# Second-half queries by seven block products (Strassen's scheme), with weight sums and split K and V kept in DRAM

## The chip, the core and the metric

The kernel runs on one core of one Trainium2 chip. The metric is the device time of one execution in microseconds (us), taken as the median of several executions. Below, PE is TensorE (the matrix engine; PEld is its loading of weights), DVE is VectorE, ACT is ScalarE, POOL is GpSimd, and SP is SyncE, which in this kernel does nothing but issue DMAs.

## What is computed

```python
def _A_ref(x, k_cache, v_cache, wq, wo):          # x: 2048 x 640; 32 heads of 128
    q = (x @ wq).reshape(B, Sq, 32, 128)...
    k = k_cache[:, :, Sk - W:, :]                 # the last W = 512 positions
    v = v_cache[:, :, Sk - W:, :]
    p = softmax(einsum("bhqd,bhkd->bhqk", q, k) * 128 ** -0.5)
    o = einsum("bhqk,bhkd->bhqd", p, v)
    return o.transpose(...).reshape(B, Sq, 4096) @ wo
def _B_ref(x, w1, b1, w2, b2):                    # 640 -> 1728 -> 640
    r = maximum(x @ w1 + b1, 0)
    return (r * r) @ w2 + b2
xn = layernorm(x)
return x + _A_ref(xn, ...) * silu(_B_ref(xn, ...))
```

All arrays are float32. Every matrix product is made from three products of a high and a low part: a = ah + al, b = bh + bl, and a·b is taken as ah·bh + ah·bl + al·bh. The high part is a copy rounded to the matrix engine's float32r (an ACT copy), the low part is the difference (a subtraction on DVE or POOL). So each 128x128 block of weights against 512 tokens costs three matmul instructions.

## The kernel before

**Stages.** The 2048 tokens are four tiles of 512. The first three go through the layer norm and the MLP (`mlp_step`, one step for each of 14 chunks of the hidden layer in each tile); the split, normalised x of all tiles is put in DRAM (`xT_d`). The MLP of the fourth tile (LATE) is done at the very end, under and behind the last attention units. Between them stands attention: 128 units, in two halves of 64. A half holds two token tiles; in it the 16 groups of two heads are gone through, and for each group the four units (token tile 0, heads 0 and 1; token tile 1, heads 0 and 1). Below, u0 to u3 are these four places, so that unit number modulo 4 is the place.

**One unit** is, on PE, 12 matmuls of scores (`s_mm`, tile s), 15 of the query of two units later (`q_mm`, tile pq; 5 chunks of the 640 inputs, three matmuls each), 12 of the weighted sum of V of the unit before (`v_mm`, tile o), and, on average, 15 of the output projection of earlier units (`r_mm`, tile r): 54.

**The loop through one unit.** The scores of a unit lie in four PSUM banks. DVE takes the maximum over the keys for each query (three folds, tile rdm); ACT gathers four strips (`gather`); DVE finishes the maximum (sqm) and turns it (rowm); SP writes the 2 KB row to DRAM (m_d) and, when that has landed, loads it back, spread over 128 partitions (bm, `row`). DVE then subtracts bm from the scores into SBUF (`shift`, tile e), which frees the banks for the scores of the next unit. ACT takes the exponential and its high part (`expo`, `p_hi`), POOL makes the low part (`p_lo`) and the sum of the two halves (`s_add`, tile su). DVE folds the sums (rds, sqs, rows), which go by DRAM as well (s_d, bs), and in the unit after next the sum of V is scaled by them (`o_norm`), split (`o_hi` on ACT, `o_lo` on DVE: tile ot) and used by `r_mm`. The o bank is single: the next `v_mm` waits for `o_lo`. A DVE instruction `r_acc` adds each projected piece to acc.

**What sets the order.** The attention's instructions are recorded in a plan: `at(when, f, ...)`, sorted by `when`, with a nominal unit (`PERIOD`) of 12.4. It sets only the order in which each engine's instructions stand; every engine then goes through its own in order. All loads and stores of the attention, m_d, bm, s_d and bs among them, are issued by SP in that one order. In a unit SP issues, in this order: m_d, bm, s_d (the sums), bs, and then loads for later units: before, two of raw weights, of 256 or 320 KB (vr, kr, qr, or for V, K and the two weights), which ACT and POOL split into high and low parts when they have landed (`load_raw`, `prep`). Each head's K, V, query weights and output weights are loaded and split in both halves, so twice in all. In units 73 to 112 `load_finish` adds one transfer of 256 KB in each unit (fs, fx, fg, then a store) for the final combination of the first half's tokens.

At the change of halves, units 60 to 64, the x of the second half's two tiles is loaded chunk by chunk (`load_xT`, tile ax).

## Time and profile before

| what | value |
| --- | --- |
| time, median of 3 runs | 1992.19 us (1991.41 to 1992.53) |
| the profiled execution | 1990.35 us, of which the span from first to last instruction is 1988.6 us |
| PE busy | 1958.7 us, 98% of the span, 8576 matmuls recorded |
| DVE, POOL, ACT busy | 1515.5 (76%), 1375.3 (69%), 1186.3 us (60%) |
| granted TensorE clock, mean | 0.999 |
| DMA | 220.39 MB, mean 111 GB/s |
| attention | first scores at 307.1 us, last unit's scores at 1879 us |

Busy time is an average over stages; in the middle of attention PE is busy without a gap. A view of the trace by stretches of time gives busy times and counts of instructions of each engine in each stretch, with the share of the 16 DMA engines' time that was busy and what they moved. The timeline lists instructions by start, each with its duration, merged where equal ones follow each other (x3), and in brackets the idle time of the engine just before and what ended it. "SPq" is SP's queue: a row there is the issue of a DMA, not its transfer.

### The profile page before, as it was taken

The numbers are of one execution on the slowest core, as the hardware profiler recorded it, in microseconds if no ns is written. First come the engines' busy times: TensorE is split into PE (matmuls) and PEld (weight loads), VectorE is DVE, ScalarE is ACT, GpSimd is POOL, SyncE is SP. The second block draws the span as 40 slices with busy tenths as digits, with TensorE's granted clock in tenths as the row PEclk, the third lists the DMA queues.
The fourth block names the chain that finished last, engine by engine and source line by source line (L and its number), as shares of the span: only waits on it lengthen the run. The fifth ranks groups of instructions, "written<-read, shape, count | busy, mean of one in ns | idle before, by whom it ended". The sixth has DMA issues, their size and how long they took to land.

```text
span 1988.6 us, 25917 instructions
## 1 busy us (share of the span) xinstructions
PE 1958.7 (98%) x8576; PEld 1603.1 (81%) x8576; DVE 1515.5 (76%) x2511; ACT 1186.3 (60%) x2034; POOL 1375.3 (69%) x755
## 2 busy tenths in 40 slices
PE   7999999999999999999999999999999999999998
PEld 6788887788888888888887788888888888888877
DVE  5523236788888888888888878888888888888864
ACT  4432326766666666666666676666666666666643
POOL 1121225888888888888887788888888888888841
PEclk9999999999999999999999999999999999999999
DMA  4421444322323233222335433333333333333354
GB/s 137 136 106 38 180 171 144 105 91 94 95 93 91 91 91 91 91 90 92 94 93 170 157 98 107 112 112 113 112 112 115 113 112 113 96 91 91 110 147 141
DMA packets 126871, 220.39 MB, mean 111 GB/s; under 512 B 21542, under 2 KB 36304, under 8 KB 125456
## 3 DMA queue, kind: packets, MB, share of 16 engines
q1 hardware_dynamic: 123744, 204.28, 32.9%
q0 software_dynamic: 2992, 14.43, 1.8%
q8 instruction: 69, 1.13, 0.2%
q14 instruction: 66, 0.54, 0.1%
HBM read 194.26 MB, written 24.39 MB: 110 GB/s over the span
## 4 chain that ended last, share of the span: by engine, by line
PE 88%; DMA 4%; DVE 4%; ACT 2%; issue 1%; POOL 1%; SPq 0%; POOLq 0%; DVEq 0%; ACTq 0%
PE pq L72 20%; PE r L72 20%; PE o L72 17%; PE s L72 17%; PE py L96 2%; PE py L97 2%; PE py L95 2%; PE ph L97 2%; PE ph L96 2%; PE ph L95 2%; PE ly L72 2%; PE lu L72 1%; DMA w1r<-in_w_dram 1%; DMA bm<-m_d 1%; DVE rdm L72 1%
## 5 line engine op out<-in xcount | busy, mean ns | idle before, releaser
L72 POOL TENSOR_TENSOR pt<-e,pt 128x1024 fp32r<-128x1024 f32 x256 | 616.2, 2407 | 120.4 <-ACT pt L72 120.4
L72 PE MATMUL r<-ot,wo 128*128 128x512 f32 x1920 | 496.9, 389 | 0.2 <-DVE acc L72 0.2
L72 PE MATMUL pq<-ax,wq 128*128 128x512 f32 x1920 | 456.6, 389 | 0.8 <-DMA ax<-xT_d 0.7
L72 PEld LDWEIGHTS pq<-ax,wq 128*128 128x128 f32 x1920 | 360.6, 188 | 76.3 <-DMA ax<-xT_d 1.5
L72 PEld LDWEIGHTS r<-ot,wo 128*128 128x128 f32 x1920 | 360.3, 188 | 75.6 <-DVE acc L72 0.6
L72 PE MATMUL s<-q,wk 128*128 128x512 f32 x1536 | 372.1, 391 | 5.9 <-DVE e L72 5.9
L72 PE MATMUL o<-pt,wv 128*128 128x512 f32 x1536 | 374.6, 392 | 1.4 <-DVE ot L72 1.2
L72 ACT ACTIVATE e<-e 128x1024 f32<-128x1024 f32 x256 | 269.9, 1054 | 126.0 <-DVE e L72 122.1
L72 PEld LDWEIGHTS s<-q,wk 128*128 128x128 f32 x1536 | 287.9, 188 | 70.7 <-issue 7.2
L72 PEld LDWEIGHTS o<-pt,wv 128*128 128x128 f32 x1536 | 283.5, 188 | 72.9 <-DVE ot L72 14.9
L72 DVE TRANSPOSE_TENSOR_REDUCE rdm<-s 128x16 f32<-128x512 f32 (+1 forms) x384 | 313.4, 868 | 36.9 <-PE s L72 36.2
L72 DVE TENSOR_TENSOR e<-s,bm 128x512 f32<-128x512 f32 (+1 forms) x384 | 304.3, 842 | 17.0 <-DMA bm<-m_d 16.8
L72 POOL TENSOR_TENSOR su<-e,e 128x1024 f32<-128x1024 f32 x128 | 307.6, 2403 | 0.0
L72 ACT ACTIVATE pt<-e 128x1024 fp32r<-128x1024 f32 x256 | 272.0, 1062 | 7.9
L237 POOL TENSOR_TENSOR r<-r 128x512 f32<-128x512 f32 (+1 forms) x42 | 44.1, 1051 | 227.9 <-ACT r L278 208.8
L72 DVE TENSOR_TENSOR acc<-r,acc 128x512 f32<-128x512 f32 x300 | 198.6, 662 | 2.7 <-PE r L72 2.7
L72 ACT ACTIVATE ot<-o 128x512 fp32r<-128x512 f32 x128 | 76.8, 600 | 197.1 <-DVE o L72 197.1
L72 ACT ACTIVATE rds<-rds 32x32 f32<-32x32 f32 x384 | 87.7, 228 | 128.5 <-DVE rds L72 125.5
L72 DVE TRANSPOSE_TENSOR_REDUCE rds<-su 128x32 f32<-128x1024 f32 x128 | 158.1, 1235 | 0.1
L72 DVE TENSOR_TENSOR ot<-o,ot 128x512 fp32r<-128x512 f32 x128 | 88.6, 692 | 85.2 <-ACT ot L72 85.2
L72 POOL TENSOR_TENSOR wv<-vr,wv 128x512 fp32r<-128x512 f32 x64 | 83.2, 1300 | 81.5 <-ACT wv L72 74.4
L72 POOL TENSOR_TENSOR wq<-qr,wq 128x640 fp32r<-128x640 f32 x62 | 97.7, 1576 | 60.2 <-ACT wq L72 60.2
(123 smaller groups left out, 2168.6 us busy)
## 6 DMA issues: line engine op xcount, KB each, us to landing
bm<-m_d SPq DMA_DIRECT2D x128, 256.0 KB, 3.2
bs<-s_d SPq DMA_DIRECT2D x128, 256.0 KB, 3.8
qr<-in_wq_dram SPq DMA_DIRECT2D x64, 320.0 KB, 4.1
or<-in_wo_dram SPq DMA_DIRECT2D x64, 320.0 KB, 4.1
kr<-in_kT_dram SPq DMA_DIRECT2D x64, 256.0 KB, 3.4
vr<-in_v_dram SPq DMA_DIRECT2D x64, 256.0 KB, 4.3
xT_d<-xT POOLq DMA_DIRECT2D x6, 1280.0 KB, 7.5
xb<-in_x_dram SPq DMA_DIRECT2D x16, 320.0 KB, 3.4
```

The lines of the kernel that those rows point to most:

```text
L72: ins = method(*args, **kwargs)
L95: nc.tensor.matmul(ps, ah, bh, start=first and i == 0, stop=False)
L96: nc.tensor.matmul(ps, ah, bl, start=False, stop=False)
L97: nc.tensor.matmul(ps, al, bh, start=False, stop=last and i == n - 1)
L237: nc.gpsimd.tensor_tensor(r, r, r, op=ALU.mult)
```

## The change

**In the second half** the 15-matmul query products are replaced. For a group, the four wanted blocks (two heads by two token tiles) over the first four chunks of the 640 inputs form a 2x2 by 2x2 block product; it is made with seven block products in place of eight (`PRODUCTS`, `part`), each of 2 chunks x 3 matmuls. The fifth chunk is added straight (four times 3 matmuls). So a group takes 54 matmuls for its queries where it took 60; over 16 groups that is 96 fewer, and 8482 in place of 8578 in the program. The factors are sums and differences of weight blocks (segments A to D, tiles ws) and of x blocks (four tiles t). The products are joined by three copies on ACT (`snap`), four additions of PSUM to SBUF on DVE (`joined`) and three on POOL (`mixed`); the split of the joined query is an ACT copy and a POOL subtraction (`joined_hi`, `joined_lo`), where before the latter was on DVE (`q_lo`, 64 of them are gone).

**In the first half** each group's weight sums are made, by five subtractions or additions of two SBUF operands on DVE (`combos`, written to cs), a copy on ACT and a subtraction on POOL (`combos_hi`, `combos_lo`), and they, the split query weights, and the split K and V of each head are stored to DRAM (`store_q`, `store_s`, `store_kv`: w_d and kv_d). The second half loads them split (`load_seg`, `load_kv`, 512 or 640 KB each) instead of loading raw and splitting anew. At the end of the first MLP the sums and differences of the x of the last two tiles are made and stored (`t_prep`: 16 POOL, 8 DVE and 8 ACT instructions on 128x512, 16 stores of 256 KB); the layer norm of the last tile is put one step earlier (`LN_AT`).

**Elsewhere**: the output weights are loaded as five pieces of 128 KB a group (`load_o`, `prep_o`); `s_add` becomes two additions within the halves, and the second `p_lo` is cut in two; e, pt, bm and bs have one buffer less; the r pieces of the second half stand at other places (`r_plan`), since its units have 51, 51, 54 and 54 matmuls; at the change of halves nine blocks of x and of its sums are loaded, in transfers of 256 or 512 KB.

SP's order, first half, from the bs of unit 32 (a u0) to the m_d and bm of unit 33 (a u1), and on to that unit's bs. Names: m_d the row of maxima and bm its copy over all partitions, s_d and bs the same of the sums; vr, qr, or raw loads of V, query and output weights; sizes in elements. Before:

```order
L72 DMA bs_6500<-s_d_6498 128x512
L72 DMA vr_17_6514<-in_v_dram 128x512
L72 DMA qr_18_6516<-in_wq_dram 128x640
L72 DMA m_d_6576<-rowm_6574 16x32
L72 DMA bm_6578<-m_d_6576 128x512
L72 DMA s_d_6626<-rows_6624 16x32
L72 DMA bs_6628<-s_d_6626 128x512
```

Now, from the bs to the m_d of unit 33 (kv_d and w_d are the new stores):

```order
L72 DMA bs_6985<-s_d_6983 128x512
L72 DMA kv_d_164<-wk_17_6846 128x1024
L72 DMA vr_17_7005<-in_v_dram 128x512
L72 DMA qr_7007<-in_wq_dram 128x640
L72 DMA w_d8A<-co_6950 256x1x256
L72 DMA w_d8B<-co_6950 256x1x256 x2
L72 DMA w_d8C<-co_6950 256x1x256
L72 DMA w_d8C<-cs_6651 256x1x128
L72 DMA m_d_7073<-rowm_7071 16x32
```

Two transfers stood between a bs and the next m_d, eight stand there now (512, 256, 320, four of 256 and one of 128 KB).

SP's order, second half, late, from the bs of unit 119 (a u3) to the m_d of unit 120 (a u0), and on. Names: as above, and wk, wv the split K and V, ws31A a segment of the weight sums. Before:

```order
L72 DMA bs_17762<-s_d_17760 128x512
L72 DMA vr_28_17776<-in_v_dram 128x512
L72 DMA or_28_17778<-in_wo_dram 128x640
L72 DMA m_d_17837<-rowm_17835 16x32
L72 DMA bm_17839<-m_d_17837 128x512
L72 DMA s_d_17888<-rows_17886 16x32
L72 DMA bs_17890<-s_d_17888 128x512
```

and now:

```order
L72 DMA bs_18725<-s_d_18723 128x512
L72 DMA or_3_18744<-in_wo_dram 128x2x128
L72 DMA wk_29_18746<-kv_d_176 128x1024
L72 DMA or_4_18753<-in_wo_dram 128x2x128
L72 DMA ws31A<-w_d15A 128x2x512
L72 DMA wv_28_18788<-kv_d_175 128x1024
L72 DMA m_d_18818<-rowm_18816 16x32
```

Two raw loads became five, 1792 KB in all.

DVE's order, second half, in unit 120 (a u0), from its folds to the split of o. Names: rdm the folded maxima of the scores s, sqm and rowm the row, acc the projected output, o and ot the sum of V and its low part. Before:

```order
L72 TENSOR_REDUCE rdm_17810<-s_0_17794 128x2x16
L72 TENSOR_REDUCE rdm_17810<-s_2_17805 128x16
L72 TENSOR_REDUCE rdm_17810<-s_3_17813 128x16
L72 TENSOR_REDUCE sqm_2330<-rdm_17810 32x16
L72 STREAM_TRANSPOSE rowm_17835<-sqm_2330 32x32
L72 TENSOR_TENSOR acc_0_11050<-r_1_17821,acc_0_11050 128x512
L72 TENSOR_TENSOR o_17764<-o_17764,bs_17762 128x512
L72 TENSOR_TENSOR ot_17847<-o_17764,ot_17847 128x512
```

Now, in the same unit (sn is a partial query in SBUF, ps the bank of the block products):

```order
L72 TENSOR_REDUCE rdm_18785<-s_0_18766 128x2x16
L72 TENSOR_REDUCE rdm_18785<-s_2_18780 128x16
L72 TENSOR_REDUCE rdm_18785<-s_3_18790 128x16
L72 TENSOR_TENSOR acc_0_11910<-r_0_18757,acc_0_11910 128x512
L72 TENSOR_TENSOR sn_7_18553<-ps_4_18708,sn_7_18553 128x512
L72 TENSOR_REDUCE sqm_2504<-rdm_18785 32x16
L72 STREAM_TRANSPOSE rowm_18816<-sqm_2504 32x32
L72 TENSOR_TENSOR o_18727<-o_18727,bs_18725 128x512
L72 TENSOR_TENSOR acc_0_11910<-r_1_18805,acc_0_11910 128x512
L72 TENSOR_TENSOR ot_18827<-o_18727,ot_18827 128x512
```

Before, the row (sqm, rowm) followed the folds at once, with one `acc` behind it; now an `acc` and a joining addition stand between the folds and the row, and the other `acc` stands between o and ot.

The core of the diff:

```diff
-                if n or kind in "vo":
-                    at(base + when - 10.5, load_raw, kind, hf, h)
-                    at(base + when, prep, kind, hf, h)
+                if hf == 0:
+                    if n or kind == "v":
+                        at(base + when - 10.5, load_raw, kind, hf, h)
+                        at(base + when, prep, kind, hf, h)
+                    if kind != "q":
+                        at(base + when + (13.6 if n or kind == "v" else 27.0 + j), store_kv, kind, h)
+                elif kind == "k":
+                    at(base + (j - 2) * PERIOD + 9.9, load_kv, kind, h)
+                elif kind == "v":
+                    at(base + j * PERIOD + 2.0, load_kv, kind, h)
...
+        if hf == 0:
+            at(base + c0, combos, g, (0,))
+            at(base + c1, combos, g, (1, 2))
+            at(base + c2, combos, g, (3, 4))
+            at(base + 6.0, combos_hi, g)
+            at(base + 9.8, combos_lo, g)
+            for j in range(G):
+                at(base + (0.0 if n == 0 else (j - 2) * PERIOD) + 2.0, store_q, g, j)
+            at(base + PERIOD + 2.0, store_s, g)
+        else:
+            for k, s in enumerate("ABCD"):
+                at(base + (k - 4) * PERIOD + 0.3, load_seg, n, s)
...
+    PRODUCTS = {
+        1: (("A", 0, ("x", 1, 0)),),
+        6: (("A", 2, ("t", 1)),),
+        7: (("B", 0, ("t", 2)),),
+        5: (("B", 2, ("t", 0)), ("B", 4, ("x", 0, 2))),
+        3: (("C", 0, ("x", 0, 1)), ("C", 2, ("x", 0, 2))),
+        4: (("C", 3, ("t", 3)),),
+        40: (("D", 0, ("x", 1, 2)),),
+        2: (("D", 1, ("x", 1, 1)), ("D", 3, ("x", 1, 2))),
+    }
...
+    def store_kv(kind, h):
+        sp.dma_start(kv_d[h][:, int(kind == "v")], raw({"k": KT, "v": VV}[kind][0, h]))
+    def load_kv(kind, h):
+        sp.dma_start(raw(open_kv(kind, 1, h)), kv_d[h][:, int(kind == "v")])
...
+            dve.tensor_tensor(out, a, b, op=ALU.subtract if k else ALU.add)
```

More of the change, by code (lines that the diff above doesn't have):

```diff
@@ L45 @@
     LATE = NTILE - 1
-    LN_AT = {t: (3, 7) if t == LATE else (5, 9) for t in range(1, NTILE)}
+    LN_AT = {t: (2, 6) if t == LATE else (5, 9) for t in range(1, NTILE)}
     SCALE = DH**-0.5
@@ L846 @@
+    at(10.0, pad, pools["ep"], 480)
+    for m, k, when in (
+        (("x", 1, 0), -4, 0.6),
+        (("t", 2), -4, 4.6),
+        (("t", 1), -4, 9.9),
+        (("x", 0, 2), -3, 0.6),
+        (("t", 0), -3, 9.9),
+        (("t", 3), -2, 0.6),
+        (("x", 1, 2), -2, 4.6),
+        (("x", 0, 1), -2, 9.9),
+        (("x", 1, 1), -1, 0.6),
+    ):
+        for i in range(2):
+            at((DU + k) * PERIOD + when + 0.1 * i, load_x, 1, m, i)
     R_AT = (
@@ L857, with r_plan @@
     R_BANK, R_BANK_END = (1, 0, 0, 1, 0), (1, 1, 1, 0, 0)
+    R_BANK_ST = (1, 0, 1, 0, 0)
+    def r_plan(i, d):
+        if i == NU - G - 1:
+            (when, js) = R_AT_END[d][0]
+            return ((when, js),), R_BANK_END[d], when + 0.68 * len(js)
+        if i + 2 < DU - 3 or i + 4 > NU - 3:
+            pieces = R_AT[d]
+            when, js = pieces[-1]
+            return pieces, R_BANK[d], when + 0.68 * len(js)
+        x = (i + 3) % UPG == 2
+        two, three, four = (k * PERIOD for k in (2, 3, 4))
+        return (
+            (((two + 11.3, range(G)),), 1, three + 3.9),
+            (((three + (4.1 if x else 3.5), range(G)),), 0, three + (5.7 if x else 5.1)),
+            (
+                ((three + (5.5 if x else 4.8), range(1)), (four + (4.8 if x else 4.1), range(1, G))),
+                1,
+                four + (5.8 if x else 5.1),
+            ),
+            (((three + 11.3, range(G)),), 0, four + 0.3),
+            (((four + (5.5 if x else 4.8), range(G)),), 0, four + (7.0 if x else 6.3)),
+        )[d]
     for i in range(NU):
@@ L889 @@
         on(PERIOD + 8.5, row, i, "s")
-        on(18.6, p_lo, i, 1)
         for c in range(KC):
```

431 lines of the change are left out of this document (321 added, 110 removed).

## The prediction

> **What bounds the kernel now.** First the page's busy times, queues and costliest groups, then the view by stretches of time, one long stretch late in the second half and one about the change of halves.
>
> ```profile
> PE 1958.7 (98%) x8576; PEld 1603.1 (81%) x8576; DVE 1515.5 (76%) x2511; ACT 1186.3 (60%) x2034; POOL 1375.3 (69%) x755
> q1 hardware_dynamic: 123744, 204.28, 32.9%
> ...
> 1046.80:1162.10 115.30, 112.16 (x488) 90.62 (x487) 94.10 (x156) 73.42 (x129) 89.37 (x46) 1.00 0.48 154
> 1608.00:1803.00 195.00, 195.00 (x858) 160.13 (x857) 167.84 (x280) 127.13 (x224) 160.47 (x82) 1.00 0.33 103
> ```
>
> PE is busy all of 195 us with 858 matmuls: 0.2273 us each, at a granted clock of 1.00. A unit of 54 takes 12.27 us. So matmuls bound the middle of attention, and fewer of them is worth time only as long as nothing else takes a unit's length. What stands next is the loop through DRAM. The timeline of a usual unit, SP and PE rows, then some of DVE's:
>
> ```profile
> 1507.79 0.32 SPq L72 DMA_DIRECT2D bs<-s_d  x1
> 1507.99 2.88 PE L72 MATMUL s<-q,wk 128*128 128x512 f32 x12
> 1508.23 0.35 SPq L72 DMA_DIRECT2D vr<-in_v_dram  x1
> 1508.63 0.43 SPq L72 DMA_DIRECT2D qr<-in_wq_dram  x1
> 1509.47 0.33 SPq L72 DMA_DIRECT2D fs<-s_d  x1
> 1513.52 0.33 SPq L72 DMA_DIRECT2D m_d<-rowm  x1
> 1514.84 0.33 SPq L72 DMA_DIRECT2D bm<-m_d  x1
> 1516.15 2.88 PE L72 MATMUL o<-pt,wv 128*128 128x512 f32 x12
> 1520.23 1.07 PE L72 MATMUL s<-q,wk 128*128 128x512 f32 x4
> ...
> 1513.29 0.20 DVE L72 STREAM_TRANSPOSE rowm<-sqm 32x32 f32<-32x32 f32 x1
> 1513.43 0.66 DVE L72 TENSOR_TENSOR o<-o,bs 128x512 f32<-128x512 f32 x1
> 1514.75 0.69 DVE L72 TENSOR_TENSOR ot<-o,ot 128x512 fp32r<-128x512 f32 x1 [0.67 <-ACT ot L72]
> 1518.38 1.77 DVE L72 TENSOR_TENSOR e<-s,bm 128x1024 f32<-128x1024 f32 x2
> ```
>
> From scores to scores 12.24 us. bm can be issued only when m_d has landed, here 1.32 us after its issue and 6.85 us after the scores began. The subtraction starts at 10.39, gives up the first two banks (1024 of the 1536 columns that the row's 1.77 us cover, 1.18) at 11.57, and PE wants them at 12.24: 0.67 us of slack. The transfers ahead of m_d here are bs and three loads, 832 KB. The DMA view gives the sizes; kr, fs and bs are of 256 KB like vr, or of 320 like qr:
>
> ```profile
> qr<-in_wq_dram SPq DMA_DIRECT2D x64, 320.0 KB, 4.1
> vr<-in_v_dram SPq DMA_DIRECT2D x64, 256.0 KB, 4.3
> ax<-xT_d SPq DMA_DIRECT2D x20, 256.0 KB, 5.0
> ```
>
> Where more stood ahead, the kernel already pays. Two units near the change of halves, one with five loads ahead (by the same view three ax, vr and or, 1344 KB), one with six (1600 KB):
>
> ```profile
> 1046.81 2.88 PE L72 MATMUL s<-q,wk 128*128 128x512 f32 x12
> 1054.72 0.32 SPq L72 DMA_DIRECT2D bm<-m_d  x1
> 1059.48 0.70 PE L72 MATMUL s<-q,wk 128*128 128x512 f32 x2 [0.20 <-DVE e L72]
> ...
> 1085.01 2.88 PE L72 MATMUL s<-q,wk 128*128 128x512 f32 x12
> 1085.20 0.86 SPq L72 DMA_DIRECT2D ax<-xT_d  x2
> 1086.34 0.33 SPq L72 DMA_DIRECT2D kr<-in_kT_dram  x1
> 1086.72 0.42 SPq L72 DMA_DIRECT2D or<-in_wo_dram  x1
> 1087.19 1.17 SPq L72 DMA_DIRECT2D ax<-xT_d  x2
> 1090.54 0.32 SPq L72 DMA_DIRECT2D m_d<-rowm  x1
> 1093.72 0.32 SPq L72 DMA_DIRECT2D bm<-m_d  x1
> 1097.16 2.42 DVE L72 TENSOR_TENSOR e<-s,bm 128x1024 f32<-128x1024 f32 x3 [1.70 <-DMA bm<-m_d]
> 1098.53 0.70 PE L72 MATMUL s<-q,wk 128*128 128x512 f32 x2 [1.12 <-DVE e L72]
> ```
>
> m_d is issued in time (in the second 5.53 us after the scores, as above) but lands behind the loads: bm goes out at 7.91 and 8.71, and the units take 12.67 and 13.52 us, bm's time plus 4.8 in both. 256 KB more cost 0.80 us, 3.1 us per 1000 KB. The queue's own row agrees: 204.28 MB in 32.9% of 1988.6 us is 312 GB/s, 3.2 us per 1000 KB. So m_d has a price list: by a usual unit's slack 832 KB are as good as free, 1344 KB cost 0.4 us and 1600 KB cost 1.25, with 3.1 us for each further 1000 KB. The Trainium skill (DMA: Bandwidth & Descriptors, Queues, rings and completion order) says that each DMA engine takes descriptors in the order of its ring; by that rule a 2 KB row waits for all that is ahead, and the trace agrees.
>
> **The change part by part.** *Matmuls.* 96 x 0.2273 = 21.8 us less on PE, all in the second half, in the places u0 and u1 (51 matmuls, 11.59 us). But there the o product stands after 33 matmuls, 7.50 us, where it stood after 36 (8.16 in the row). It needs the o bank: ot ends 7.45 us after the scores in the rows above (1515.44), with only one `acc` between the folds and the row. In u0 two additions stand there, and in u1 two come ahead of the folds; of 0.6 us each, the gather's gap takes most, some 0.25 stays. So the product starts about 7.94 (ot's end at 7.7, and the load of weights behind it), 0.44 late, in 31 units: +13.6. Left of the saving: 8 us.
>
> *SP's queue, first half.* By the order, the transfers between a bs and the next m_d are 1024 KB in u0, 2240 in u1, 1728 in u2 and 1664 in u3; before, 576. From the 1600 KB unit: u1 has 640 KB more, 2.0 us, so bm at 10.7 and a unit of 15.5 (+3.2). u2 would be 13.9, but a long u1 lets bs and the loads start some 1.5 us earlier against u2's scores: +0.1. u3: 13.7 (+1.4). u0: nothing. Sum 4.7 for four units. One unit is little ground, and the stores of K and V move 4 KB a row, which may drain faster than 2; with 1 us less in u1 and u3 the sum is 2.5 or so. Nearest is the 1600 KB row, for u3 nearly the same load, so I keep between the ends: 3.6. Units 5 to 59 are 13.75 such fours: 49 us (34 to 65). No cover is left, since the slack is used before.
>
> *DVE against POOL, first half.* The five `combos` read two SBUF operands each and stand between the folds and the row. Such an operation is seen beside POOL here:
>
> ```profile
> 326.89 2.41 POOL L72 TENSOR_TENSOR pt<-e,pt 128x1024 fp32r<-128x1024 f32 x1
> ...
> 328.14 1.71 DVE L72 TENSOR_TENSOR eh_g<-lr,eh_x 128x512 fp32r<-128x512 f32 x1
> ```
>
> It takes 1.71 us and ends 0.55 after POOL's (329.30), where DVE's o and ot above, of the same 128x512, take 0.66 and 0.69. So it waits for the running POOL operation, up to 2.4 us. The Trainium skill (SBUF — State Buffer, SBUF: two separate sides) calls this an exclusive lock between GpSimd and a VectorE operation with two SBUF inputs; the row agrees. In u3 the wait lies under the queue's, in u2 under slack; in u0 it shows. I take 0.5 us for four units, 7 us (0 to 27: 2 us). POOL itself gets 45.4 us of work in four units of 49.1, against 40.4. With 2.41 for 1024 columns from the row above, this one gives the scale, 2.16 us per 1000 columns and 0.2:
>
> ```profile
> L72 POOL TENSOR_TENSOR wv<-vr,wv 128x512 fp32r<-128x512 f32 x64 | 83.2, 1300 | 81.5 <-ACT wv L72 74.4
> ```
>
> (Four `p_lo` of 2.41 and eight halves of 1.30, eight sums of 1.30, raw weights 8.4, five pieces of 256 columns at 0.75, and 2.9 for the low part of the weight sums.) It fits, a u0 that runs 1 us over being made good in u1; cost nothing, and up to 1 us a four if that cover is gone.
>
> *SP's queue, second half.* Ahead of m_d stand 1792 KB in u0, 1152 in u1, 768 in u2, 1280 in u3. u0: bm at 8.71 + 0.6 = 9.3, unit 14.1, 2.1 over the 12.0 that the o bank gives. u3: +0.25. With the finish transfers of 256 KB (10 of 15 fours) u0 gets 2.5 (0.8 more, less 0.4 since u3 is longer) and u3 1.05; I take off 0.25 for what 832 KB cost before. That is 2.35 or 3.3; with 0.7 to 1 us less, 1.4 or 1.9. Middle: 1.9 x 5 + 2.6 x 10 = +35 (26 to 45).
>
> *The rest.* Change of halves, units 60 to 64: 18.7 MB are queued in place of 9.5, 9.2 x 3.1 = 28 us of transfer, of which about half falls into time in which the queue stood idle (0.48 busy there before): +12 (3 to 25). First units, where 2176 to 2752 KB stand ahead of m_d three times: +5 (0 to 10). `t_prep`: POOL gets 5.2 us (four of 1.30) a step of 30 matmuls, 6.8 us, beside its square: +2 (0 to 8). ACT has a third of its time free, and the single buffers of bm and bs are free in time by the rows above: nothing.
>
> Sum: -21.8 + 13.6 + 49 + 7 + 35 + 12 + 5 + 2 = +102. The profiled execution took 1990.35 us, which gives 2092; the median of the runs stands 1.84 above it: **2094 us**. The ends, added up (with half of the o wait at the low one): 2040 and 2164.
>
> By the skill's ceiling of 435 GB/s for the 16 engines (same page, Specifications), 2.3 us per 1000 KB, u1 of the first half would be 0.5 shorter and the estimate some 10 us lower; no stretch of this trace shows that rate.
>
> **The rivals.** *The queue hides it* (faster): if the larger rows drain so fast that up to 2.2 MB pass ahead of m_d in the slack, only PE and the o bank count: 1992 - 8 = 1984. It decides at m_d's landing by 7 us. For it: even about the change of halves the engines are idle for half the time (0.48 busy for 154 GB/s). Against: in that very stretch 1600 KB put bm at 8.71. 10%.
> *Half-way* (slower): only u1 in the first half and u0 in the second pay, 1 us each: 1992 - 8 + 14 + 15 + 8 = 2021. For it: the price list rests on two units. Against: the queue's own rate gives the same price. 15%.
> *POOL becomes the bound*: if the lock stalls POOL as well, its 45.4 us grow past the longer fours (52.7) and e and pt, with two buffers, hold back the subtraction: each `combos` then costs its full 2.4, 12 us a four, 165 us more than I count, about 2250. Only one row shows the lock in attention. 6%.
>
> **How the numbers follow.** The forecast, 2040 to 2164, has 69%. The range takes in most of the half-way case and cuts the top: 2010 to 2150. Runs here differ by 1 us, so 0.2% (4 us) is about what can be told from no change. Faster 0.10, the first rival; the same 0.02, the border of the two; slower 0.88.
>
> **What would show it.** Right: bm issued 9 us or more after the scores in u1 (first half) and u0 (second half), waits of DVE's e for bm as in the row of 1097.16 (1.70 us) in two of four units, PE's s waiting for e, and 3 to 5 us per four in the first half, where no matmul changed. Wrong: units of 12.3 us in the first half, or PE waiting for something else than the scores' banks (o, q or x).

## The result and the profile after

The changed kernel takes 2195.19 us (median of 4 runs, 2186.64 to 2196.84), the kernel before beside it 1991.8 (1990.9 to 1992.53): 1.1013 times as long, 95% interval 1.0984 to 1.1042. The forecast was 2094, range 2010 to 2150: the direction held, the size was half of what came. The profiled execution after took 2186.64 us, the fastest of its four runs (the other three lie between 2194 and 2197); its span is 2184.9 (1988.6 before), 196.3 longer.

Where they went is read off the starts of the units' scores in the timeline (the last column, "tail", is unit 126 to the end):

| stage, us | to first scores | units 0-4 | 5-59 | 60-63 | 64-125 | tail |
| --- | --- | --- | --- | --- | --- | --- |
| before | 307.1 | 63.5 | 676.2 | 51.7 | 766.1 | 123.9 |
| after | 326.8 | 67.9 | 765.3 | 82.8 | 815.5 | 126.6 |
| difference | +19.7 | +4.4 | +89.1 | +31.1 | +49.4 | +2.7 |
| forecast | +2 | +5 | +56 | +12 | +27 | 0 |

The page after: busy times, the queue, and three groups of instructions with the idle time ahead of them.

```profile
PE 2003.5 (92%) x8480; PEld 1590.5 (73%) x8480; DVE 1622.5 (74%) x2599; ACT 1183.1 (54%) x2122; POOL 1516.4 (69%) x1171
q1 hardware_dynamic: 222656, 326.99, 46.7%
L72 PE MATMUL s<-q,wk 128*128 128x512 f32 x1536 | 391.9, 405 | 86.8 <-DVE e L72 64.1
L72 DVE TENSOR_TENSOR e<-s,bm 128x512 f32<-128x512 f32 (+1 forms) x384 | 306.6, 850 | 109.1 <-DMA bm<-m_d 108.8
L72 DVE TRANSPOSE_TENSOR_REDUCE rds<-su 128x32 f32<-128x1024 f32 x128 | 158.1, 1235 | 13.1 <-POOL su L72 13.1
```

By the view of stretches, units 5 to 59, 60 to 63 and 64 to 125 after (columns: length, then busy time of PE, PEld, DVE, ACT and POOL with instructions, granted TensorE clock as a share of the full one, DMA share, GB/s):

```profile
394.70:1160.00 765.30, 703.33 (x2971) 553.46 (x2971) 652.87 (x1024) 462.79 (x846) 616.95 (x454) 0.99 0.50 162
1160.00:1242.80 82.80, 59.92 (x230) 46.14 (x229) 45.52 (x73) 33.02 (x61) 45.84 (x36) 0.88 0.64 216
1242.80:2058.20 815.40, 764.04 (x3240) 604.81 (x3241) 657.25 (x1087) 478.78 (x880) 668.07 (x507) 0.99 0.48 154
```

No engine and not the DMA engines are busy throughout: in the first stretch PE is at 92%, DVE at 85%, POOL at 81%, the DMA engines at 50%. So this is waiting, not work. PE now idles, mostly for DVE's subtraction, and that for bm. (The clock of 0.88 in units 60 to 63 is taken up below.) The wait for bm was forecast; but it is 109 us, and not all of it is the queue's. Unit 32, a u0 (scores at 772.6), DVE and POOL in the timeline:

```profile
776.62 1.00 DVE L72 TENSOR_TENSOR cs<-qr,cs 128x256 f32<-128x256 f32 x1
777.54 1.38 DVE L72 TENSOR_TENSOR cs<-qr 128x128 f32<-128x128 f32 x1
778.84 0.40 DVE L72 TENSOR_REDUCE sqm<-rdm 32x16 f32<-32x256 f32 x1
779.27 0.20 DVE L72 STREAM_TRANSPOSE rowm<-sqm 32x32 f32<-32x32 f32 x1
...
774.92 2.42 POOL L72 TENSOR_TENSOR pl<-e,ph 128x1024 fp32r<-128x1024 f32 x1
777.28 1.49 POOL L72 TENSOR_TENSOR su<-e 128x512 f32<-128x512 f32 x1
778.73 2.59 POOL L72 TENSOR_TENSOR pl<-e,ph 128x512 fp32r<-128x512 f32 x2
```

The first sum ends at 777.62, 0.28 after POOL's operation (777.34); the second, half its size, begins while POOL's next one runs and ends 0.15 after that (778.92 against 778.77). So the row is finished at 6.85 us after the scores in place of 5.5, m_d goes out 1.35 late with an idle queue, and the unit takes 13.64. SP's queue in the unit behind it, a u1 (scores at 786.3):

```profile
786.24 0.32 SPq L72 DMA_DIRECT2D bs<-s_d  x1
786.61 0.42 SPq L72 DMA_DIRECT2D kv_d<-wk  x1
...
789.78 1.28 SPq L72 DMA_DIRECT2D w_d8B<-co  x2
...
792.58 0.78 SPq L72 DMA_DIRECT2D m_d<-rowm  x1
796.64 0.33 SPq L72 DMA_DIRECT2D bm<-m_d  x1
```

bm can go out only 4.06 us after m_d (1.34 in unit 32), at 10.3 in the unit (10.7 was forecast), and the unit takes 15.12. So u1 is the queue's, as foreseen, and u0 the sums'. The signs named in the prediction came: in the mean bm goes out 10.3 us after the scores in u1 of the first half and 9.2 in u0 of the second. But the first half lost 6.5 us per four units, not 3 to 5.

### The profile page after: what moved, and what is told of

Read it like the earlier page. It is cut to its first block, busy times and chain, and to the rows that moved or that the text cites. A ratio compares the mean times of both kernels' runs of the same rounds, so it can differ in the third digit from the quotient of the medians.

```text
span 2184.9 us, 27264 instructions
## 1 busy us (share of the span) xinstructions
PE 2003.5 (92%) x8480; PEld 1590.5 (73%) x8480; DVE 1622.5 (74%) x2599; ACT 1183.1 (54%) x2122; POOL 1516.4 (69%) x1171
## 4 chain that ended last, share of the span: by engine, by line
PE 26%; DVE 23%; DMA 20%; POOL 12%; issue 10%; ACT 7%; SPq 2%; POOLq 0%; ACTq 0%; DVEq 0%
DMA m_d<-rowm 7%; DMA bm<-m_d 7%; DVE rdm L72 6%; DVE e L72 5%; POOL pl L72 5%; PE o L72 4%; PE s L72 4%; PE r L72 3%; POOL su L72 2%; ACT e L72 2%; DVE acc L72 2%; PE ps L72 2%; PE ly L72 2%; ACT rdm L72 2%; SPq L72 1%
## 5 line engine op out<-in xcount | busy, mean ns | idle before, releaser
L72 POOL TENSOR_TENSOR pl<-e,ph 128x512 fp32r<-128x512 f32 (+1 forms) x384 | 637.8, 1675 | 2.6 <-ACT ph L72 2.2
L72 PE MATMUL s<-q,wk 128*128 128x512 f32 x1536 | 391.9, 405 | 86.8 <-DVE e L72 64.1
L72 POOL TENSOR_TENSOR su<-e 128x512 f32<-128x512 f32 x256 | 342.2, 1337 | 174.8 <-ACT e L72 174.4
L72 PE MATMUL o<-ph,wv 128*128 128x512 f32 x1024 | 346.8, 400 | 39.1 <-DVE ot L72 38.7
L72 ACT ACTIVATE ph<-e 128x1024 fp32r<-128x1024 f32 x256 | 271.8, 1062 | 7.9
L72 PEld LDWEIGHTS o<-ph,wv 128*128 128x128 f32 x1024 | 193.8, 189 | 102.9 <-DVE ot L72 63.8
L72 PE MATMUL pq<-ax_x,wq 128*128 128x512 f32 x960 | 228.1, 389 | 0.3 <-ACT sn L72 0.3
L72 PEld LDWEIGHTS pq<-ax_x,wq 128*128 128x128 f32 x960 | 180.1, 188 | 38.2 <-ACT sn L72 0.7
L72 PE MATMUL o<-pl,wv 128*128 128x512 f32 x512 | 203.6, 398 | 3.0 <-POOL pl L72 2.5
L72 ACT ACTIVATE rds<-rds 32x32 f32<-32x32 f32 x384 | 87.5, 228 | 162.6 <-DVE rds L72 158.3
L72 POOL TENSOR_TENSOR wo<-or,wo 128x256 fp32r<-128x256 f32 x160 | 117.1, 741 | 75.5 <-ACT wo L72 75.4
```

The costliest lines, as they stand in the source:

```text
L72: ins = method(*args, **kwargs)
```

## The experiments

The theory at the start: the row is late by its place on SP's queue, behind the bulk transfers, and by the lock between POOL and DVE's operations with two SBUF operands (`combos` in the first half, `t_prep` before it). Rivals: the engines' memory traffic as such, on whatever queue; in the second half, DVE's order; at the change of halves, what SP waits for. All figures are from one profiled run each, stages as above.

| run | time | to first scores | 0-4 | 5-59 | 60-63 | 64-125 |
| --- | --- | --- | --- | --- | --- | --- |
| after | 2186.64 | 326.8 | 67.9 | 765.3 | 82.8 | 815.5 |
| e1 row on ACT's queue | 2196.1 | 329.3 | 70.5 | 768.6 | 77.3 | 821.7 |
| e2 no sums | 2185.05 | 327.3 | 68.4 | 754.9 | 87.5 | 818.1 |
| e5 no stores | 2145.24 | 325.4 | 66.5 | 729.0 | 74.8 | 821.2 |
| e6 neither | 2102.64 | 327.2 | 64.5 | 685.5 | 76.1 | 821.5 |
| e9 stores behind bm | 2166.68 | 327.8 | 69.3 | 738.2 | 83.8 | 820.1 |
| e10 and sums moved | 2211.74 | 328.9 | 70.7 | 774.6 | 85.1 | 824.6 |
| e7 no K, V loads | 2155.78 | 327.9 | 67.6 | 766.5 | 86.1 | 778.7 |
| e8 acc later | 2187.3 | 328.6 | 68.2 | 769.3 | 85.6 | 807.1 |
| e11 loads behind bm | 2192.88 | 327.6 | 68.3 | 770.2 | 84.2 | 815.0 |
| e3 layer norm back | 2191.99 | 320.1 | 70.9 | 768.9 | 85.4 | 819.4 |
| e4 t_prep on DVE | 2185.59 | 313.5 | 68.8 | 773.8 | 82.6 | 819.2 |
| e13 no x loads | 2179.62 | 329.3 | 68.1 | 764.5 | 70.1 | 819.3 |
| e17 first segments later | 2194.54 | 329.1 | 67.8 | 774.3 | 82.5 | 813.6 |
| e18 both of these | 2170.98 | 326.5 | 67.4 | 766.6 | 58.6 | 823.9 |
| e12 all moves | 2172.99 | 308.1 | 71.1 | 780.9 | 73.3 | 811.4 |
| e16 four moves | 2137.69 | 309.0 | 69.8 | 738.1 | 84.4 | 808.4 |
| before | 1990.35 | 307.1 | 63.5 | 676.2 | 51.7 | 766.1 |
| e14 before, K, V stores | 2006.78 | 307.2 | 65.3 | 683.9 | 58.4 | 767.0 |
| e15 before, sums | 2116.68 | 307.1 | 70.4 | 791.4 | 54.1 | 767.4 |

In runs whose edit doesn't touch them, units 5 to 59 take 764.5 to 774.3 us and units 64 to 125 813.6 to 824.6, and after lies near the low end of both; smaller effects there are not read.

### First half: what the queue is, and the two causes

**e1, a queue of its own for the row.**

```diff
-        sp.dma_start(d, r)
+        (act if what == "m" else sp).dma_start(d, r)
...
+        on(5.2, spread, i, "m")    # bm, also from act, behind o_hi
```

> The row of maxima (m_d) and its copy (bm) are issued by ACT, on a queue of its own; everything else stays on SP. Nothing is left out. Queue theory (the bulk transfers ahead of m_d on SP's queue make it late): bm goes out about 7 us after the scores everywhere the row is in time, so u1 of the first half falls from about 15 to 12.4, u2 from 13-14 to 12.4, u0 and u3 stay at 13.6 and 13.2 (their row itself is late); units 5 to 59 fall from 765 to about 710 us. Second half: u0 from 12.7-15.4 to about 12.4 and u3 from 12.8-14.4 to 12.4, units 64 to 125 from 815 to about 768. Units 60 to 63 from 83 to 55-65 (bs stays behind the loads). In all about -130 us, 2060. Rival (the engines' memory traffic as such is the limit, not the place in the queue): m_d lands as late as before on any queue, and the time stays within 20 us of 2187. Lock theory alone (POOL and DVE hold each other up): units 5 to 59 stay above 750.

Not so: 2196 in place of 2060, and units 5 to 59 and 64 to 125 as they were. The row's issue in a u1 of e1, in the timeline, and the landings of m_d in units 5 to 59 of e1 and of after (the view of the tile rowm):

```profile
852.68 0.33 ACTq L72 DMA_DIRECT2D m_d<-rowm  x1
...
856.54 0.34 ACTq L72 DMA_DIRECT2D bm<-m_d  x1
```
```profile
DMA to landing us min/median/max: 1.3/2.8/4.8
```
```profile
DMA to landing us min/median/max: 1.3/1.7/4.1
```

A queue of its own doesn't let the row pass; the backlog in front of the 16 engines holds it up from another queue as well. The Trainium skill (DMA: Bandwidth & Descriptors, Queues, rings and completion order) says that an engine takes turns between the rings that have work, a whole packet of descriptors each turn; by that rule the row would wait for about one turn. No run here shows the turns themselves; what the trace shows is that the row of this unit is followed by bm only after 3.86 us, on a queue of its own, where m_d lands after 1.3 us at the least.

**e2, e5 and e6, the causes left out one by one and together.**

```diff
-            dve.tensor_tensor(out, a, b, op=ALU.subtract if k else ALU.add)   # e2, e6: raw weights copied instead
+            pass
...
+        if h >= G: return      # e5, e6: store_kv; store_q, store_s: if g: return
```

> Leaves out the five weight sums on DVE (combos): the segments are made from the raw weights instead, so all copies, POOL work, stores and loads stay as they are, and the second half computes with wrong factors. Lock theory (the sums wait for POOL between the folds and the row): the row is finished at 5.5 us in every unit, u0 of the first half falls from 13.65 to 12.3, u3 from 13.3-14 to about 12.6; units 5 to 59 from 765 to 730-735, u1 and u2 stay at 14-15.5 and 12.4-14. Queue theory alone (the sums only take their own 1.9 us, under cover): less than 10 us. The prediction's value for this was 7 us. Units 64 to 125 unchanged within 5 us.

> Leaves out the first half's stores of split K and V, query weights and sums after the first group; the second half loads as many bytes, but always those of the first group, so its result is wrong. The sums on DVE stay. Backlog theory (what counts is how many bytes stand in front of the DMA engines, whatever the queue): bm goes out at about 7 us in u1 and u2, which fall to 12.3-12.5; u0 stays at 13.7 and u3 at 13.0-13.3, since there the row itself is late (lock). Units 5 to 59 from 765 to about 710 us. If the lock were only cover for the queue, u0 and u3 would fall as well and units 5 to 59 come near 680. Units 60 to 63 from 83 to about 70; units 64 to 125 as before, about 816.

> Leaves out both the stores after the first group and the five sums on DVE. Backlog and lock together (each fills the place that the other leaves): all four units at 12.3, units 5 to 59 at 676-682 us, as in the kernel before, so 87 of the 89 us go here while the sums alone took away 10. If POOL's larger work (45 us in four units) were a third cause, units 5 to 59 stay above 690. Units 64 to 125 about 816.

Without the sums 10 us go (hardly more than runs differ; 30 to 35 were expected), without the stores 36 (55 were expected), without both 80. Each lies over the other. DVE's wait for bm, in the groups of the stretch from 400 to 1040 us, of after, e2, e5 and e6 in this order:

```profile
L72 DVE TENSOR_TENSOR e<-s,bm 128x1024 f32<-128x1024 f32 x46 | 55.0, 1195 | 32.6 <-DMA bm<-m_d 32.5
```
```profile
L72 DVE TENSOR_TENSOR e<-s,bm 128x1024 f32<-128x1024 f32 x46 | 55.5, 1207 | 55.2 <-DMA bm<-m_d 55.1
```
```profile
L72 DVE TENSOR_TENSOR e<-s,bm 128x1024 f32<-128x1024 f32 x49 | 57.5, 1173 | 1.1 <-DMA bm<-m_d 1.0
```
```profile
L72 DVE TENSOR_TENSOR e<-s,bm 128x1024 f32<-128x1024 f32 x52 | 61.4, 1181 | 2.6 <-DMA bm<-m_d 2.6
```

In e2 u0 falls from 13.75 to 12.54 in the mean and u3 by 0.6, but the wait for bm rises by 23 us: u1 and u2 give back 0.5 each, and bm of u1 goes out 10.7 us after the scores in place of 10.3. That the shorter unit leaves the stores less time fits this, but no run shows it by itself. Read from the bottom, the sums alone add 43.5 (e5 less e6), the stores alone 69.4 (e2 less e6). By place, the sums alone add 1.4 us in u0 and 1.8 in u3, and nothing in u2: there the row of e5 is finished 5.6 us after the scores, as in e6. e6 stays 9 us above before, nearly all in u1 (12.84 in the mean, 12.25 before); there DVE's sum fold waits for POOL, in the waits of e6's units 5 to 59:

```profile
DVE rds L72 <- POOL su L72: 12.2, 14, 1.1
```

14 times, once in four units: POOL has the low part of the weight sums (2.42 and 0.46 us) ahead of su. That is 0.65 us for four units, where the prediction counted nothing for POOL, "and up to 1 us a four if that cover is gone".

**e15 and e14, each cause alone in the kernel before.**

```diff
+        for k in ks:   # e15: (2,), (2, 2), (2, 1) at 3.9 in u2, u3, u0
+            dve.tensor_tensor(CS[0][:, :k, :], a[:, :k, :], b[:, :k, :], op=ALU.add)
...
+            sp.dma_start(kv_d[h][:, int(kind == "v"), i], src)   # e14
```

> The kernel before, with five DVE operations of the sums' sizes added between the folds and the row in u2, u3 and u0 (one, two and two; high and low part of a query weight as operands, an unused result), and bm in one buffer for the room; nothing else. Lock theory, with the size that the difference between the two runs without stores gave: units 5 to 59 from 676 to 715-725 us (+43), u0 and u3 by 1.4 and 1 to 1.8, u2 less. By their own 0.3 us each, under the slack of the row, less than 10. The prediction's value was 7 (0 to 27).

> The kernel before, with the stores of split K and V alone added in the first half, at the places of the changed kernel (two of 256 KB a unit, ahead of m_d); nothing is left out and nothing reads them. By the prediction's price list (832 + 512 KB ahead of m_d cost 0.4 us a unit) units 5 to 59 go from 676 to about 698 us; if stores are dearer or cheaper than loads, outside 688-708. Second half unchanged at 766.

The sums alone cost 115 us, over twice the lock theory's figure. A u3 of e15 (scores at 918.2), DVE and POOL in the timeline:

```profile
922.74 4.98 DVE L72 TENSOR_TENSOR cs<-wq,wq 128x256 f32<-128x256 f32 x2
927.64 0.40 DVE L72 TENSOR_REDUCE sqm<-rdm 32x16 f32<-32x256 f32 x1
...
920.15 2.41 POOL L72 TENSOR_TENSOR pt<-e,pt 128x1024 fp32r<-128x1024 f32 x1 [0.63 <-ACT pt L72]
922.51 2.40 POOL L72 TENSOR_TENSOR su<-e,e 128x1024 f32<-128x1024 f32 x1
924.86 2.57 POOL L72 TENSOR_TENSOR pt<-e,pt 128x1024 fp32r<-128x1024 f32 x1
```

Two sums take 4.98 us, one POOL operation of 1024 columns each; the row is finished 10.0 us after the scores. u3 takes 17.9 to 19.2 from unit 11 on, u0 14.7 in the mean. u1 and u2 stay at 12.24 and 12.31, so neither the single buffer of bm nor the one sum in u2 costs anything. The changed kernel has cut POOL's additions and a `p_lo` into 512 columns (1.30), and there a sum takes 1.0 to 1.4 in the median. So what such a DVE operation takes goes by the POOL operation that it meets, not by its own length (in the timeline of after 0.37 us at the least for 128x256, 0.27 for 128x128). The stores of K and V alone cost 8 us in units 5 to 59, not 22: 512 KB more in every unit is 0.14 us, not 0.4. Whether the price list is too steep there or stores are cheaper than the loads that it was read from, no run tells.

**The clock beside these causes.** The lock is not all of e15's 115 us. In its long u3 the sum of V is late too, since DVE frees the o bank behind the row. PE stops for it, and the granted clock is 0.50 around the end of that stop; the 12 matmuls of o, 2.88 us in the prediction's timeline, take 5.49. PE in the timeline, then the view of the stretch from 929.1 to 935.9 us (the clock stands third from the end):

```profile
930.27 5.49 PE L72 MATMUL o<-pt,wv 128*128 128x512 f32 x12 [3.72 <-DVE ot L72]
```
```profile
929.10:935.90 6.80, 5.63 (x13) 4.51 (x14) 5.93 (x10) 4.27 (x9) 2.81 (x2) 0.50 0.15 49
```

u3 is 17.9 us where the clock is at 0.50 for 3.4 us, and 18.6 to 19.2 where it is for 6.8. In units 5 to 59 the mean granted clock was 1.000 in before, e5, e6, e9 and e14, 0.991 in after, 0.977 in e2, 0.974 in e10 (below) and 0.948 in e15. Times the length of the stage, what was missing is at most 7, 17, 20 and 41 us, an estimate, as PE does not set the pace all the time. So the 43.5 us of e5 less e6 are free of it; the 69.4 of the stores and e15's 115 hold some of it, and no run takes it apart.

**e9 and e10, other places.**

```diff
-                        at(base + when + (13.6 if n or kind == "v" else 27.0 + j), store_kv, kind, h)
+                        u = j + 1 if kind == "v" or n == 0 else j - 1
+                        at(base + u * PERIOD + 4.3, store_kv, kind, h)
...
+                    at(base + u * PERIOD + 9.9, combos, g, (k,))   # e10: u = -1, -1, 0, 0, 0
```

> In the first half the stores of split K and V, query weights and sums stand behind bm in SP's order (between bm and s_d) in place of ahead of m_d. Same bytes, nothing left out; the sums stay in the row's path. Backlog theory (only what stands in front of the DMA engines when m_d is issued counts): as without the stores, u1 12.9, u2 12.5, u0 13.7, u3 13.3-14, units 5 to 59 from 765 to 728-738 us. Rival (the bytes have to move in any case, and bs and the raw loads then come late in m_d's place): above 755 us. Second half unchanged.

> As the run before (stores behind bm), and the five sums stand directly ahead of DVE's subtraction in u3 (two) and u0 (three), where POOL waits for its next e; nothing is left out. Lock theory: they take 0.3-0.4 us each instead of 1.0-1.5, the row is finished at 5.5 in every unit, u3 is 12.3 and u0 12.7 (three sums, 0.9 us, against 0.5 of slack); units 5 to 59 at 690-700 us, close to 685 without stores and sums. If POOL is busy there as well and the lock strikes again, the sums delay e instead of the row and the time stays at 728-745.

e9 does as expected in sum: 738, with the same bytes; u1 is 12.9, and m_d's median landing in units 5 to 59 is 1.3 us again, as before the change. But u2 stays at 13.5, where 12.5 was expected, so the stores are not free there. e10 fails: 775. The sums met POOL at the new place too, here in unit 40 in the timeline of e10:

```profile
898.68 0.79 DVE L72 TENSOR_TENSOR cs<-qr 128x256 f32<-128x256 f32 x1
899.39 1.50 DVE L72 TENSOR_TENSOR cs<-qr,cs 128x256 f32<-128x256 f32 x1
900.82 0.81 DVE L72 TENSOR_TENSOR cs<-qr 128x128 f32<-128x128 f32 x1
901.55 2.40 DVE L72 TENSOR_TENSOR e<-s,bm 128x1024 f32<-128x1024 f32 x3
...
899.14 1.47 POOL L72 TENSOR_TENSOR wv<-vr,wv 128x512 fp32r<-128x512 f32 x1
900.57 0.91 POOL L72 TENSOR_TENSOR wo<-or,wo 128x256 fp32r<-128x256 f32 x1
```

POOL splits weights there, and the sums hold up e itself, where no slack is left. Up to 20 of the 36 us above e9 can be the clock's, by the estimate above.

### Second half

```diff
+        if h >= G: home[1, h] = home[1, h % G]; return          # e7: load_kv
-            (((three + 11.3, range(G)),), 0, four + 0.3),
+            (((three + 11.3, range(G)),), 0, four + 2.9),       # e8: r_acc behind the folds
-                at(base + (k - 4) * PERIOD + 0.3, load_seg, n, s)
+                at(base + (k - 5) * PERIOD + 8.3, load_seg, n, s)  # e11; load_kv: 9.9 to 8.2, 2.0 to 4.3
```

> Leaves out the second half's loads of split K and V after the first group (every group uses the first group's); the segments, output weights and finish transfers stay. Ahead of m_d stand 1280 KB in u0, 640 in u1, 256 in u2, 768 in u3 or so. Backlog theory: u0 from 13.7 to about 12.5, u3 from 13.4 to 12.3, and what is left over matmuls is DVE's order (u1 and u2 stay at 12.35); units 64 to 125 from 815 to 765-775 us. Rival (DVE's and PE's order is what makes the second half long): less than 20 us. First half as it was, 765.

> In the second half the addition acc that stands ahead of the folds in u1 and u3 is put behind them, into the gap in which DVE waits for ACT's gather; nothing is left out. DVE-order theory: in those u1 that are not late by the queue the folds start at 1.6 in place of 2.2, and the unit falls from 12.35 to about 11.8, the length of its 51 matmuls plus the wait for the o bank; with half of the u1 and u3 units free of the queue, units 64 to 125 from 815 to 803-810 us. If the length of u1 is set by DVE's whole work (11 us of 12.35 busy) or by the o bank, less than 3 us. First half unchanged.

> In the second half the loads of the segments and of split K and V stand behind bm in SP's order, earlier by up to half a unit than before; same bytes, nothing left out. Backlog theory: ahead of m_d only bs, output weights and the finish transfers are left, under 832 KB, so u0 falls from 13.7 to 12.1-12.4, u3 from 13.4 to 12.4, u1 and u2 stay at 12.35 by DVE's order; units 64 to 125 from 815 to 765-772 us. Rival (the bytes count wherever they stand, since s_d and bs then come late and the o bank with them): above 795.

The loads of K and V are worth 37 us: without them u0 is 12.43 in place of 13.71. That is a little short of what was expected (765 to 775): 778.7 is still above before's 766.1, with 96 matmuls fewer. Unit 97 of after, a u1 without delay by the queue (scores at 1675.8), DVE in the timeline:

```profile
1676.78 0.68 DVE L72 TENSOR_TENSOR acc<-r,acc 128x512 f32<-128x512 f32 x1
1677.37 0.68 DVE L72 TENSOR_TENSOR sn<-ps,sn 128x512 f32<-128x512 f32 x1
1677.97 2.43 DVE L72 TRANSPOSE_TENSOR_REDUCE rdm<-s 128x32 f32<-128x1024 f32 x3
1681.26 0.41 DVE L72 TENSOR_REDUCE sqm<-rdm 32x16 f32<-32x256 f32 x1 [0.85 <-ACT rdm L72]
...
1686.66 0.20 DVE L72 STREAM_TRANSPOSE rows<-sqs 32x32 f32<-32x32 f32 x1
1686.80 2.37 DVE L72 TENSOR_TENSOR e<-s,bm 128x1024 f32<-128x1024 f32 x3
```

DVE's chain, not PE's 51 matmuls (11.59), is the length of the unit: 12.35. With acc in the gap of 0.85 (e8) such units are 11.9, and the stage is 8 us shorter, about what the theory said. 807 and e16's 808, with the same move, lie below all of the runs that keep this stage as it is (813.6 to 824.6). e11 brought nothing in sum: bm goes out earlier (7.6 us after the scores in u0, 9.2 in after), but it lands later, with the loads issued right behind it. Its landing in e11's units 64 to 125 (tile view; after has 3.0/3.1/3.4):

```profile
DMA to landing us min/median/max: 3.1/4.0/4.9
```

So "behind bm" is no free place for loads of 512 and 640 KB in every unit.

### Before the first scores

```diff
-    LN_AT = {t: (2, 6) if t == LATE else (5, 9) for t in range(1, NTILE)}
+    LN_AT = {t: (3, 7) if t == LATE else (5, 9) for t in range(1, NTILE)}   # e3, t_prep at steps 9, 10
-            nc.gpsimd.tensor_tensor(s, raw(xs[0])[:, cc, :], ...)
+            nc.vector.tensor_tensor(s, raw(xs[0])[:, cc, :], ...)   # e4, and lo too
```

> The last tile's layer norm starts one step later again, at 3 and 7 as in the kernel before, and t_prep with it (steps 9 and 10). If DVE's wait of 7.8 us for xb, which holds up the hidden layer's splits behind it, comes from the earlier start, PE's 4.5 us of idle time at 210 to 230 us goes and the first scores come about 5 us earlier (322 in place of 327). If it does not, or if t_prep then collides with the end of the stage, the first scores stay within 2 us of 327 or come later. Attention unchanged.

> t_prep's 16 POOL operations are put on DVE, so that no POOL work of t_prep runs beside DVE's operations with two SBUF operands; DVE gets 16 x 0.69 = 11 us more over the stage. Lock theory: DVE operations there take 0.69 again in place of 1.4 to 3.5, and PE's 12 to 14 us of idle time between 250 and 290 us shrink to a few; first scores at about 315 in place of 327. Rival (plain work in DVE's order, no lock): DVE's extra 11 us stand ahead of the hidden layer's splits just the same and the first scores stay at 325 or later. Attention unchanged.

Both hold: -6.7 and -13.3 us, and together (e12) the first scores are at 308.1. The two waits, in after's timeline of DVE and then POOL:

```profile
226.04 0.89 DVE L72 BATCH_NORM_STATS2 st<-xb 128x6 f32<-128x320 f32 x2 [7.77 <-DMA xb<-in_x_dram]
...
257.73 3.48 DVE L246 TENSOR_TENSOR h<-r,h 128x512 fp32r<-128x512 f32 x1 [1.59 <-ACT h L245]
...
255.54 1.49 POOL L244 TENSOR_TENSOR r<-r 128x512 f32<-128x512 f32 x1
256.98 1.14 POOL L72 DMA_DIRECT2D xT_d<-xT  x2
258.13 2.51 POOL L358 TENSOR_TENSOR to<-tr,to 128x512 fp32r<-128x512 f32 x2
```

A split of the hidden layer, 0.69 us by itself, took 3.48: it ended 0.57 after two POOL operations in a row, though it had begun 0.40 before the first. On DVE, the 11 us of work cost 1 to 2 us (308.1 in e12 and 309.0 in e16 against before's 307.1). e4 takes away two things at once that no run takes apart: the lock, and the time that POOL's square (r, for which ACT and then the split wait) stands behind `t_prep` on POOL. And the clock is in both prices: from 150 us to the first scores PE stood idle for 14.1 us in after, 7.6 in e3 and 3.2 in e4 (before: not at all), and the granted clock was 0.50 for 17.0, 10.2 and 3.4 us.

### Change of halves

```diff
+        if hf: X[1, m] = X[0, HOLD[m]]; return                  # e13, e18: load_x
-                at(base + (k - 4) * PERIOD + 0.3, load_seg, n, s)
+                at(base + (k - 4) * PERIOD + (8.3 if first else 0.3), load_seg, n, s)  # e17, e18: A, B of group 16
```

> Leaves out the loads of x and of its sums at the change of halves (8 MB in units 60 to 63); the second half computes with the first half's x instead. Backlog theory: units 60 to 63 fall from 83 to 54-58 us (the K, V and segment loads and the last stores of the first half stay). Rival (the stores of the last group and SP's waits for buffers are what is long): above 70. All other stages unchanged.

> The loads of the second half's first two segments stand behind bm of units 60 and 61 instead of ahead of m_d, so SP doesn't wait for PE's last query products with m_d queued behind; the x loads stay, nothing is left out. SP-wait theory: units 60 to 63 from 83 to 70-75 us. If the x loads fill the place (8 MB in four units): above 79.

> The same, and the loads of x and of its sums left out (wrong x in the second half). If the x loads and SP's wait are the two causes: units 60 to 63 at 56-60 us, against 70 with the x loads alone left out and 52 in the kernel before. If a third cause is there: above 64.

Without the x loads 13 of the 31 us go, not 25. What stayed is in SP's rows of e13's unit 61 (scores at 1178.5), timeline, and in its waits of 1161 to 1202 us:

```profile
1178.15 0.38 SPq L72 DMA_DIRECT2D vr<-in_v_dram  x1
1188.89 0.32 SPq L72 DMA_DIRECT2D ws16B<-w_d0B  x1
...
1193.35 0.56 SPq L72 DMA_DIRECT2D m_d<-rowm  x1
```
```profile
SPq L72 <- PE pq L72: 15.1, 2, 10.3
```

SP stands for 10.3 us until PE has read the query weights whose buffer the segment takes, and m_d, whose row is finished at 1186.4, stands behind it and behind five stores of the last group's sums, which take another 4.1 us to issue. Moved alone (e17), the segments bring nothing; with the x loads left out as well (e18) 24 of the 31 us are gone and that wait with them. Again two causes, each under the other; the last 7 us stay open.

The clock is in these 31 us too. Three times PE stops for 5.5 to 6.5 us, and each time the granted clock is 0.50 for 6.8 us. Unit 62 of after, PE in the timeline:

```profile
1204.81 5.46 PE L72 MATMUL s<-q,wk 128*128 128x512 f32 x12 [5.50 <-DVE e L72]
```

The scores take 5.46 us in place of 2.88, and the row is finished 7.7 us after their start in place of 5.5. In the stage the mean granted clock was 0.88 in after, 0.93 in e13 and 1.00 in e18 and before; by the estimate used above that is at most 10 of the 31 us, and no run takes it apart from the waits that lead to the stops.

### Together

e12 is e3, e4, e8, e10, e11 (its first two segments as in e17) and the x loads behind bm; e16 is e3, e4, e8 and e9.

> All the moves together, nothing left out: the layer norm one step later, t_prep on DVE, stores and second-half loads behind bm, the sums ahead of the subtraction, acc behind the folds, and at the change of halves the loads of x and of its sums behind bm too. If the causes add up by stages: first scores at 307-310 us, units 0 to 4 66, units 5 to 59 about 695, units 60 to 63 60-70 (8 MB still have to come in four units), units 64 to 125 757-765, tail 126: 2010 to 2035 us, still slower than before by 1 to 2 per cent. If the gains are worth less together, 2050 or more.

> The changed kernel with the four moves that helped alone: the layer norm one step later, t_prep on DVE, the first half's stores behind bm, acc behind the folds; the sums, the second half's loads and the x loads stay where they were, nothing is left out. If the parts add: 2187 - 20 (first scores at 307-308) - 27 - 8, about 2130 us, still 7 per cent slower than before. If they don't, above 2145.

e12: 2169.49 us (2164.06 to 2172.99), 1.0885 times before (1.0866 to 1.0904); the first scores came as forecast. Little else did: the first half lost it by the moved sums, as in e10 (781 us, forecast 695), units 64 to 125 stayed at 811 (757 to 765) and units 60 to 63 at 73 (60 to 70). e16: 2136.86 us (2135.8 to 2140.38), 1.0728 (1.071 to 1.0746). The four moves add up stage by stage (309, 738, 808), and the kernel is still 145 us slower than before.

## Why the prediction was wrong

**The step that failed** is "DVE against POOL": 7 us (0 to 27), because "in u3 the wait lies under the queue's, in u2 under slack; in u0 it shows. I take 0.5 us for four units". The row of the lock was read rightly, and so was the slack of u2; the size in u0 and u3 was not. The sums stand between the folds and the row, and in u0 and u3 they meet POOL at work, so that each takes what is left of a POOL operation. Shown, with the clock at 1.000 in both runs (e5 less e6): 1.4 us in u0 and 1.8 in u3, 3.2 for four units in place of 0.5, and 43.5 us in place of 7. In the kernel before, beside POOL operations of twice the length, the sums cost 115, a part of it the clock's. "Under the queue's wait" held for some of u3's share (with the stores there, leaving out the sums shortens u3 by 0.6), but the two causes overlap in the same wait and could not be added as 49 + 7.

It is the largest of the missed terms, not the only one: with 43.5 in its place the forecast would be 2130 us, still 65 below the result.

**Where +102 fell short of +196**, 94 us, by stage: first half 33 (the sums above), second half 22, change of halves 19, before the first scores 18, tail 3, first units -1.

- *SP's queue, first half*, +49 (34 to 65): measured 36 on top of the sums, 69 without them (the latter with a part of the clock's). Size about right, and bm of u1 as forecast (10.3 for 10.7). The price list was right for 2.2 MB in one unit and too steep for 0.5 MB of stores in every unit (e14). That the row waits because of its place on SP's ring was not borne out: another ring doesn't help (e1), another time does (e9).
- *POOL*, nothing: 9 us, in u1 alone, where its order makes DVE wait. The rival that it becomes the bound did not come: it is busy for 81% of the stage.
- *t_prep*, +2 (0 to 8): 13.3, by the lock and by POOL's order, which no run parts; and the step of the layer norm, 6.7, was in the diff but had no term at all.
- *Change of halves*, +12 (3 to 25): 31. The bytes were counted, but not the wait that a load adds to its queue: what is queued behind SP is m_d.
- *Second half*: the K and V loads (37) are near the +35 forecast for the whole queue, and bm of u0 goes out at 9.2 for 9.3. The saving of matmuls less the o bank, -8, did not come: in u1 two DVE additions ahead of the folds, priced at 0.25 us by the bank, make DVE the unit's length. Of the 49 us, 37 and 8 are shown by e7 and e8, each by itself; that they add there was not run, and what each part of the rest is stays open.
- *The clock* had no term. It was 0.999 in the mean before and 0.982 after; times the span that is at most 39 us in place of 2, an estimate, and it lies inside the terms above, as it followed PE's stops.

The two faster or smaller rivals fell by u1 of the first half alone: it is 2.6 us longer in the mean, where the first gives it nothing and the second 1 us.

## What to carry over

Ask of every instruction that a change puts on a loop's critical path which other engine it can lock with there, and price it by that engine's longest operation, not by its own duration. When two causes delay the same row, price each with the other left out: alone in the changed kernel they read 10 and 36 us, together 80. Look at the granted clock before a difference is put down to one wait: a stop of PE can be paid for twice. And list for each queued transfer not only its bytes but what it waits for, since a small urgent one stands behind that wait as well.

## What the runs showed of the hardware

- A VectorE operation on 128x256 with two SBUF operands, 0.37 us at the least, took 2.46 to 2.54 us beside 128x1024 POOL operations (e15's u3 from unit 11 on), and 1.0 to 1.4 in the median in the changed kernel, which has cut some of them to 128x512. One of 128x512 (0.69) outlasted two POOL operations in a row (3.48 us). The Trainium skill's exclusive lock (SBUF — State Buffer, SBUF: two separate sides) says which operations collide; these are the prices seen here.
- A 2 KB row issued on a queue of its own, into 16 engines with a backlog from another queue, landed after 2.8 us in the median, against 1.7 on the shared queue and 1.3 with the backlog moved elsewhere (e9).
- A 256 KB copy over the partitions landed after 4.0 us in place of 3.1 when 512 to 640 KB were issued right behind it on the same queue.
- In e15 PE stopped for 3.7 to 3.8 us in each u3 from unit 11 on, and around the end of each of these 13 stops the granted clock was 0.50 for 3.4 or 6.8 us; the 12 matmuls of o behind it took 4.3 to 5.5 us in place of 2.88.
